# Token sums by six loads, turned norms' last features doubled by DMA, and a new instruction order

## The chip, the cores and the metric

The kernel runs on one core of a Trainium2 chip. The metric is device time in microseconds (us) of one execution; the time before is a median of 681.16 us over three runs (681.0 to 682.04).

## The reference

One transformer block over 2048 tokens of 448 features, float32 in and out: a layer norm, sliding-window attention with 16 heads of 28 features, the residual, a second layer norm, a gated feed-forward of 1792, and the residual.

```
qkv = layernorm(x) @ wqkv                     # 16 heads, Dh = 28
scores = q k^T * Dh**-0.5, kept where 0 <= i - j < 256
h = x + (softmax(scores) v) @ wo
n = layernorm(h)
out = h + (gelu(n @ w_gate) * (n @ w_up)) @ w_down
```

## The kernel before, in words

**Arithmetic.** Each matrix product is made from a high part (the value rounded to the matmul's short float32 form, `to_hi`, on ScalarE, ACT) and a low part (the rest, `to_lo`, a subtraction on VectorE, DVE, or GpSimd, POOL). The features lie on partitions: 448 of them are three blocks of 128 and one of 64, and the fourth block holds the last 64 features' high and low parts one above the other, so that one product is 11 matmuls (`TERMS`) rather than 12 or more.

**Stages.** Tokens come in 16 tiles of 128. Stage one normalises each tile (`layer_norms`, kind `ln1`), transposes it on TensorE (PE), and makes values (`wv`) and queries and keys (`wqk`, `project`); these go to DRAM and return as the operands of the scores in the tile `ring`. Attention runs over blocks of queries: matmuls into PSUM banks (`scores`), a row maximum on DVE (`maxima`), exponentials on ACT (`probs`), a mask on POOL (`select`), products with the values (`attend`), the output weights (`wos`, `ohl`) and the residual (`drain`). There are 256 scores, counted from 0 below, and 16 groups of `attend`.

**The second norm.** `normalise` with kind `ln2` goes through `turn`: DVE transposes 32x32 blocks, four DMAs write the tile to a DRAM scratch (`xn_d`) as features by tokens, and for tiles 0 to 7 two loads bring it back to `xT`, blocks 4 to 6 and block 3. ACT then makes the high parts and POOL (tiles 0 to 3, `TURNED`) or DVE the low parts.

**The feed-forward.** A part of it is done by plain products (`conv`: 22 matmuls of gate and up, a gelu `ge` on ACT, a product on DVE at L1115, high and low parts; `down`: products with the down weights into four banks, which DVE adds to `hres`, L1069). The other part multiplies sums of token tiles with sums of weight columns. `combine(p, i, key)` builds those token sums for a pair of tiles, 4 apart in a half p: it loads both tiles' features from `xn_d` into two scratch rows of blocks `T[0]` (four blocks) and `T[1]` (six), adds and subtracts blocks on DVE (`add`, L460) and writes high parts (`parts_of`, ACT) and low parts (`sub`, DVE, L254) of the sums `X` and `XL`. Pairs 0 to 3 (p = 0) are built while `conv` runs; PE uses the first sum at 360.35 us of the profiled execution.

**Order.** Nothing is scheduled by hardware or by the compiler. Every operation is recorded in `Lists.op` with its engine and what it reads and writes; `play` then emits all of them in an order that the table `PLAN` gives, a packed list of numbers. Each engine, and the DMA queue of SyncE (SP), works through its own list in that order and waits on semaphores, so what stands behind a waiting instruction on its engine waits too. `cost` and `lat` in `op` and `dma` feed only the search that made the table.

Names of tiles in the rows below: `bank_134` to `bank_141` are PSUM banks; `xT`, `ring`, `proj`, `v`, `raw`, `mask` are stretches of SBUF that different stages share; `xn_118` to `xn_133` are the DRAM scratch of the turned tiles 0 to 15.

Of the kernel before, what the change touches and what calls it, by code (L numbers as in the profile page):

```python
# [13 lines left out]
OP = mybir.AluOpType  # L14
# [38 lines left out]
MOVED = 0  # L53
# [82 lines left out]
def block_kernel(ctx: ExitStack, tc, x, wqk_in, wv_in, wo_in, ffn_in, halves_in, out):  # L136
# [57 lines left out]
    last_hi = ring_m[:, 10240:10368]  # L194
# [108 lines left out]
    def normalise(t, key, kind):  # L303
        moved = kind == "ln2" and t >= MOVED
        i2, i4 = (t % 2 if t > 7 else 1) if moved else t % 2 if t < 4 else 1, t % 4
# [44 lines left out]
    def turn(t, key, i2):  # L350
# [8 lines left out]
        if t > 7:  # L359
            return  # L360
        put = [("xnd", t, a) for a in range(4)]
        dma(key + 0.1, 230, lambda: nc.sync.dma_start(f(xT[:, 4:7, c]), d[0:384].rearrange("(b p) t -> p b t", p=128)),
            put, [XT(t)])
        dma(key + 0.1, 80, lambda: nc.sync.dma_start(f(xT[:, 3, c]), d[D - 128:D]), put, [("xt3", t)])

        eng = nc.gpsimd if t in TURNED else nc.vector
# [10 lines left out]
        op("act", 1.1, 1.2, key + 0.2, hi, [("xt3", t)], [XT(t), span("ring", 10240, 128)])  # L377
        op("pool" if t in TURNED else "dve", 1.6 if t in TURNED else 0.8, 1.7 if t in TURNED else 0.88, key + 0.2, lo,
           [XT(t), span("ring", 10240, 128)], [XT(t)], port=True)
# [35 lines left out]
    def combine(p, i, key):  # L415
# [17 lines left out]
        def some(src, *ks):  # L433
            return src[128 * ks[0]:128 * ks[0] + 64 * ks[1]].rearrange("(k p) t -> p k t", k=ks[1])

        for k in range(2):
            t = 8 * p + 4 * k + i
            d, put = xn_d[t], [("xnd", t, a) for a in range(4)]

            def load(rows, lo, n, src, part, k=k, put=put):  # L440
                dma(key, (64 if rows.stop - rows.start == 128 else 32) * n, lambda: nc.sync.dma_start(  # L441
                    T[k][rows, 128 * lo:128 * (lo + n)].rearrange("p (k t) -> p k t", k=n), src), put,
                    [("Th", p, k, part), *at(k, *range(lo, lo + n))])
# [22 lines left out]
        def parts_of(q, src, r, n, key):  # L466
# [21 lines left out]
        add(128, b(1, 2, LOW), at(1, 2), b(0, 2, LOW), at(0, 2), b(1, 4, LOW), at(1, 4), key + 1)  # L488
# [114 lines left out]
    def wqk_split(m):  # L603
# [3 lines left out]
        op("dve", 0.6, 0.7, key, lambda: to_lo(wqk[i][:, 1], wqk_raw[m % 2], wqk[i][:, 0]),  # L607
# [367 lines left out]
    def term(p, j, name, a):  # L975
# [5 lines left out]
        return R[part][:, w, wb], lambda: X(p, q)[:, xb] if xb < 2 else XL(p, LO_OF[q][xb - 2])[:, 0], XS(p, q, xb) + at(part, w, 1, (wb,))  # L981
# [330 lines left out]
    "c-pPEW3(nc)HWEWQb-|H)wXThwr$(CZQHhO+qP|M`t3gbeBaEPHS=TU)Vh;OvT^Mzd)G-IV1NS*2%x{;!0#6Re*Zg$zgOVz2mg^lzklp^3xBsb"  # L1312
    ";sJkt;P>p`(Z8PjmO_7Y|Mvf*`9F64XM`f=z@IVrqrv_>e<kRj+5gd?zvcdVq`xhKKYqy{fAG&d_@e{<=;J@=(VsQ&#}bH`!4adstLRUBC;}b("
    "^Ts3Q!5=2je~3W@A{^o4A8zy;5B{^lBY631`7h?bT;T})e+Xa%p1-`I2#J3&|K)}KLBjsnA%A55vGw;4|B-=zbpKia5%Gfv6fDB~|M2l||NgS|"
    "KNd-ZZ~n)_U%7wU@ITxC=6D1LID$P8p^YODvOl}b{`g=KdkZ4?<PrS;;|NArVi7U&h*kQ>Cye0kACG^v@E@(eZ}^W5{9h)q2(;{v^k1BR{qX<d"
    "LJ^vOc_k6~0wP-YM;1i1C_?X_#9vNW1bg&9-#8-w!5_~&Vt@X|^)LHb1S$~W8AovPH>=Q}>fjL>{=a83`rqmR{KpB7u!$n_@b6y!MT8=%^RHF@"
    "pG6oE`~Rv}9<fh2B9H&^#Utv1L~zCa%To~H^<U5b+t<Ij@h^-1Y0!uo{2MQb(EJx2`mf?yM2-IA|6gUI{~`o`kdg>Ie>wP97dT@4@4NE9zC-^a"
    "XAy7w4@d03JwtzTfJWrsUo_;uYK0Ni^|$|Da{p=#{9jg3#J3Cn;g0@qasS`R{h#gqzsvuBk^49L|4$x+1i$-4zelnDjAH+hiV4yIA4CD^L2?iS"
    "WcaO>0;B{PL0k|55b6K<$plh?tRMiXL1vH*WCtcl403`jzx^f!X+REOf!zNW8}&ea&;T?9jX-121SABxKw1zL<oUgn1pEqrg_S^MPz6*4)j)Mn"
    "1JneyKwgj^L<btk_j|nni1xc}3Yvj}AQ@-{T7x#AEocV{f%c#S=m<K2=AZ@W3~GaEunuSmx`1w=JE#kKfS#ZX=mn<3K|p}PU<jB2b<i6O1riJc"  # L1320
    "rNM9z8O($ufB{B=S#T5>4HiQei~*Cu6fhPng;T*aP!UWA6Tmny8_obT!7Q)@T6i`X4+?`hU@ox1GS~-5+!xG&^MLa^>Ls8U=n9sCg<w8h2Ihn1"
# [174 lines left out]
```

## Time and profile before

| | us |
|---|---|
| median of three runs | 681.16 |
| the profiled execution | 680.14 |
| its span, first to last instruction | 678.4 |
| PE busy | 665.5 (98%) |
| DVE busy | 504.8 (74%) |
| ACT busy | 396.8 (58%) |
| POOL busy | 299.9 (44%) |
| DMA moved | 89.66 MB, 132 GB/s on average |

The profile shows one execution of the program. An engine is busy while it executes; the spans of matmuls overlap, since they are pipelined, and their ends are modelled. PEld is TensorE's loading of weights, which runs ahead of the matmuls. SPq is SyncE's queue, which issues all DMAs of this kernel. In the chain of waits each piece is the work to which the next piece had to wait, followed back from the last instruction. Stages by time: first norm and projections from 8.97 us, first score at 41.08, last `attend` up to 306.69, first sum used at 360.35, and the feed-forward without a gap from 374 to 674.

### The profile page before, as it was taken

The page shows a single profiled execution, that of the slowest core. Times are in us where ns is not written, and L with a number is a line of the kernel's source. Part 1 is how long each engine was busy: PE and PEld are TensorE (multiplying, and loading weights), DVE is VectorE, ACT ScalarE, POOL GpSimd, SP SyncE. Part 2 cuts the span into 40 slices and gives each one's busy share as a digit, 9 for nine tenths or more (in the row PEclk, how much of TensorE's full clock was granted, in tenths as well). Part 3 has the DMA queues.
Part 4 walks back from the last instruction along what each step waited for, and adds up shares of the span by engine and source line. Part 5 has one row for each costly group of instructions (what it writes and reads, how often), then busy time and mean ns, then how long its engine had stood idle before and what let it go on. Part 6 is the DMA issues. An engine that isn't in the chain of part 4 may idle for free.

```text
span 678.4 us, 11973 instructions
## 1 busy us (share of the span) xinstructions
PE 665.5 (98%) x4074; PEld 592.7 (87%) x4074; DVE 504.8 (74%) x1278; ACT 396.8 (58%) x765; POOL 299.9 (44%) x459
## 2 busy tenths in 40 slices
PE   8999999999999999999989999999999999999997
PEld 7998878888889877778878999999999999999997
DVE  7898789977688979977988899876566355545554
ACT  5766578774867698886455655634554443433431
POOL 3632524543444488756433474256554442122200
PEclk9999999999999999999998999999999999999999
DMA  7888866464747687544534434121212201101202
GB/s 268 267 254 250 265 185 210 140 213 135 236 131 255 180 210 221 125 119 105 150 98 95 102 85 128 57 91 39 67 53 70 74 15 52 52 7 62 110 0 109
DMA packets 92951, 89.66 MB, mean 132 GB/s; under 512 B 35225, under 2 KB 82009, under 8 KB 92889
## 3 DMA queue, kind: packets, MB, share of 16 engines
q1 hardware_dynamic: 92888, 88.89, 44.2%
q8 instruction: 32, 0.52, 0.3%
q14 instruction: 31, 0.25, 0.1%
HBM read 59.51 MB, written 29.36 MB: 131 GB/s over the span
## 4 chain that ended last, share of the span: by engine, by line
PE 88%; DVE 7%; DMA 2%; issue 1%; ACT 1%; SPq 1%; POOL 0%; DVEq 0%; ACTq 0%
PE bank L248 81%; PE bank L798 6%; DVE bank L692 2%; DVE v L460 1%; DMA v<-xn 1%; PE bank L314 1%; DMA pp<-in_wv_dram 1%; DVE xT L254 1%; DVE X L254 1%; SPq L441 0%; DVE proj L254 0%; PE bank L719 0%; DVE hres L1069 0%; DVE mhl L712 0%; DVE xn L823 0%
## 5 line engine op out<-in xcount | busy, mean ns | idle before, releaser
L248 PE MATMUL bank<-xT,proj 128*128 128x512 f32 x620 | 171.1, 384 | 0.0
L692 DVE CUSTOM_DVE_ANT_0 bank<-bank,mask 128x384 f32<-128x384 f32 (+2 forms) x256 | 131.6, 551 | 24.0 <-PE bank L248 22.0
L248 PE MATMUL bank<-ring 84*128 84x384 f32 (+6 forms) x618 | 136.3, 311 | 2.4 <-DVE mx L692 1.0
L248 PE MATMUL bank<-xT,ring 128*128 128x512 f32 x536 | 134.8, 379 | 0.0
L248 PE MATMUL bank<-ring,proj 128*128 128x448 f32 x628 | 128.9, 356 | 2.5 <-DVE hres L1069 2.5
L248 PEld LDWEIGHTS bank<-ring,proj 128*128 128x128 f32 x628 | 119.6, 190 | 5.8 <-ACT xT L251 2.9
L248 PEld LDWEIGHTS bank<-xT,proj 128*128 128x128 f32 x620 | 113.6, 190 | 11.4 <-DVE mhl L709 0.2
L766 ACT ACTIVATE pp<-bank 128x384 f32<-128x384 f32 (+1 forms) x212 | 103.3, 533 | 21.6 <-PE bank L248 18.4
L248 PEld LDWEIGHTS bank<-ring 128*128 128x128 f32 (+1 forms) x618 | 103.5, 190 | 13.7 <-DVE mx L692 2.4
L248 PEld LDWEIGHTS bank<-xT,ring 128*128 128x128 f32 x536 | 101.1, 189 | 13.1 <-DVE v L1013 0.6
L779 POOL TENSOR_SCALAR_AFFINE_SELECT pp<-pp 128x512 f32<-128x512 f32 x120 | 73.9, 642 | 56.1 <-ACT pp L766 55.2
L1069 DVE TENSOR_TENSOR hres<-bank,hres 128x448 f32<-128x448 f32 x72 | 42.7, 618 | 33.0 <-PE bank L248 32.9
L248 PE MATMUL bank<-proj,xT 128*128 128x224 f32 x352 | 60.8, 274 | 0.3 <-ACT proj L251 0.2
L937 POOL TENSOR_TENSOR raw<-raw 64x128 f32<-64x128 f32 (+1 forms) x90 | 48.3, 549 | 28.7 <-DMA raw<-in_halves_dram 25.4
L254 DVE TENSOR_TENSOR proj<-v,proj 128x512 fp32r<-128x512 f32 (+1 forms) x56 | 40.2, 725 | 23.9 <-ACT proj L251 23.5
L248 PEld LDWEIGHTS bank<-proj,xT 128*128 128x128 f32 x352 | 52.9, 191 | 2.3 <-ACT proj L251 0.7
L251 ACT ACTIVATE proj<-v 128x512 fp32r<-128x512 f32 (+1 forms) x56 | 32.8, 601 | 36.0 <-DVE v L1039 32.4
L254 POOL TENSOR_TENSOR ring<-raw,ring 128x256 fp32r<-128x256 f32 (+2 forms) x42 | 38.3, 920 | 35.2 <-ACT ring L251 34.5
L251 ACT ACTIVATE ring<-bank 8x512 fp32r<-8x512 f32 x64 | 37.4, 585 | 26.8 <-PE bank L719 25.5
L1013 DVE TENSOR_TENSOR v<-v,bank 128x512 f32<-128x512 f32 x48 | 32.8, 684 | 26.2 <-PE bank L248 23.6
L248 PE MATMUL bank<-wos,ohl 128*128 128x448 f32 x192 | 49.4, 359 | 0.3 <-DVE mx L692 0.2
L248 PE MATMUL bank<-X,ring 128*128 128x512 f32 x146 | 48.2, 379 | 0.0
(117 smaller groups left out, 955.7 us busy)
## 6 DMA issues: line engine op xcount, KB each, us to landing
ring<-k SPq DMA_DIRECT2D x44, 336.0 KB
raw<-in_halves_dram SPq DMA_DIRECT2D x18, 640.0 KB
ring<-q SPq DMA_DIRECT2D x32, 336.0 KB
q<-proj SPq DMA_DIRECT2D x15, 448.0 KB
k<-proj SPq DMA_DIRECT2D x11, 448.0 KB
hres<-in_x_dram SPq DMA_DIRECT2D x16, 224.0 KB
xn<-xn SPq DMA_DIRECT2D x64, 56.0 KB
ge<-in_halves_dram SPq DMA_DIRECT2D x16, 224.0 KB
```

The lines of the kernel that those rows point to most:

```text
L248: nc.tensor.matmul(o.rearrange("p (t h) -> p t h", h=2), w, mixed(m), **how)
L251: nc.scalar.activation(dst, src, AF.Copy)
L254: (eng or nc.vector).tensor_sub(dst, src, f(hi))
L314: nc.tensor.transpose(bank[b.k][:, n * 128:(n + 1) * 128], xn[i2][:, o:o + 128], ident)
L460: op("dve", 0.07 + n * 0.00104, 0.17 + n * 0.00104, key, lambda: nc.vector.tensor_tensor(out, a, b, op=op_), [*ar, *br, "mtfree"], w, port ...
L692: nc.vector.tensor_tensor_reduce(at, at, plain(mask[:, o:384]), 1.0, -BIG, OP.add, OP.max, mx[i // 2][:, i % 2, j:j + 1])
L766: nc.scalar.activation(pp[:, j:j + per, o * 128:o * 128 + n].rearrange("p j (h t) -> p j h t", h=2), bank[b.k][:, 0:n * per].rearrange("p ...
L779: nc.gpsimd.affine_select(a, a, pattern=[[0, 4], [-cm, 128]], compare_op=op_, fill=0.0, base=0, channel_multiplier=cm)
L798: nc.tensor.matmul(bank[b.k][32 * j:32 * j + DH + 1, lo * 128:(hi + 1) * 128], v[:, 4 * c - 2 + m, g % 2, j, :], pp[:, j, at[m] * 128:(at[ ...
L937: op("pool", 0.14 + n * 0.00215, 0.18 + n * 0.00215, key, lambda: nc.gpsimd.tensor_tensor(out, a, b, op=OP.subtract), [*ar, *br], w, port= ...
L1013: op("dve", 0.605, 0.702, key, lambda: nc.vector.tensor_tensor(plain(out), plain(a), unmixed(bank[bs[i].k]), op=OP.add), ar, w, bs[i])
L1069: op("dve", 0.533, 0.626, key + 3 * q + 3, lambda t=t, b=banks[q]: nc.vector.tensor_tensor(plain(hres[:, t, :]), unmixed(bank[b.k][:, 0:D] ...
```

## The change

1. `combine` loads a pair of tiles by six DMAs instead of eight. Features 0 to 383 come by one load of three blocks, and the last 64 features come twice, onto both halves of the partitions, by one load whose source repeats (`twice`). The blocks in `T` change places for it, and so do the weights' rows on the host (`four`) and the order of `X`'s two blocks (`1 - xb`).
2. In `turn` the last 64 features are loaded twice, onto 128 partitions, into 128 columns of `ring`; the high parts of block 3 are then one ACT instruction instead of two.
3. The low parts of the first value weights (`wv_split`, p = 0) and of the first query and key weights (`wqk_split`, m = 0) are made on POOL instead of DVE.
4. `MOVED` goes from 0 to 16 with the test turned round: as before, all tiles of `ln2` take `turn` and none of `ln1` does. The costs in `dma` change, and the table `PLAN` is a new one. 26 warm-up matmuls stand in it instead of 30; the other matmuls are the same.

```diff
     def normalise(t, key, kind):
-        moved = kind == "ln2" and t >= MOVED
+        moved = kind == "ln2" or t >= MOVED
...
     def turn(t, key, i2, kind):
...
-        dma(key + 0.1, 80, lambda: nc.sync.dma_start(f(xT[:, 3, c]), d[D - 128:D]), put, [("xt3", t)])
+        dma(key + 0.1, 80, lambda: nc.sync.dma_start(last, d[D - 64:D][None].to_broadcast([2, 64, 128])), put, [last_at])
...
         def hi():
             to_hi(xT[:, 0:3, c], f(xT[:, 4:7, c]))
-            to_hi(last_hi[64:128], f(xT[64:128, 3, c]))
-            to_hi(xT[0:64, 3, c], f(xT[64:128, 3, c]))
+            to_hi(xT[:, 3, c], last)
 
         def lo():
             to_lo(xT[:, 4:7, c], f(xT[:, 4:7, c]), xT[:, 0:3, c], eng)
-            to_lo(xT[64:128, 3, c], f(xT[64:128, 3, c]), last_hi[64:128], eng)
+            to_lo(xT[64:128, 3, c], last[64:128], xT[64:128, 3, c], eng)
...
     # combine
-            load(slice(0, 128), 0, 2, d[0:256].rearrange("(k p) t -> p k t", k=2), 0)
-            last = d[384:448].rearrange("(k p) t -> p k t", k=1)
-            if not k:
-                load(LOW, 2, 2, some(d, 2, 2), 1)
-                load(HIGH, 2, 2, some(d, 2, 3)[:, 0::2], 2)
-            else:
-                load(LOW, 3, 1, some(d, 2, 2)[:, 1:2], 1)
-                load(LOW, 4, 2, some(d, 2, 2), 2)
-                load(HIGH, 4, 2, some(d, 2, 2), 3)
-                load(HIGH, 2, 2, last.to_broadcast([64, 2, 128]), 4)
+            def twice(r):
+                return d[r:r + 64][None].to_broadcast([2, 64, 128])
+            load(slice(0, 128), 1 + 2 * k, 3, d[0:384].rearrange("(k p) t -> p k t", k=3), 0)
+            load(slice(0, 128), 0, 1, twice(384), 1)
+            if k:
+                load(HIGH, 1, 2, d[0:128].rearrange("(k p) t -> p k t", k=2), 2)
+                load(LOW, 1, 1, d[0:64], 3)
...
-        add(128, b(1, 0), at(1, 0), b(0, 0), at(0, 0), b(1, 0), at(1, 0), key + 1)
+        add(128, b(1, 4), at(1, 4), b(0, 2), at(0, 2), b(1, 4), at(1, 4), key + 1)
...
     # wv_split, for p = 0, and wqk_split, for m = 0
-            op("dve", 0.54, 0.63, key + 1, lambda b=b: to_lo(wv[:, 1, b:b + 2], wv_raw[p][:, b:b + 2], wv[:, 0, b:b + 2]),
+            eng, name = (nc.vector, "dve") if p else (nc.gpsimd, "pool")
...
 PLAN = (
-    "c-pPEW3(nc)HWEWQb-|H)wXThwr$(CZQHhO+qP|M`t3gbeBaEPHS=TU)Vh;OvT^Mzd)G-IV1NS*2%x{;!0#6Re*Zg$zgOVz2mg^lzklp^3xBsb"
...
```

**PE, the end of attention.** Between the last two groups of `attend` (`bank<-pp,v`), before; `bank<-ring` are scores, `bank<-xT,proj` are 512-column matmuls of the feed-forward that need no exponential.

```order
L248 MATMUL bank_135<-ring 128x384
L248 MATMUL bank_141<-xT,proj 128x512
L248 MATMUL bank_135<-ring 128x384
L248 MATMUL bank_137<-ring 128x384
L248 MATMUL bank_134<-ring 128x384
L248 MATMUL bank_140<-ring 128x384
L248 MATMUL bank_135<-xT,proj 128x512 x11
L798 MATMUL bank_139<-pp,v 29x128 x4
L798 MATMUL bank_139<-pp,v 29x256 x4
L798 MATMUL bank_139<-pp,v 29x384 x8
L798 MATMUL bank_139<-pp,v 29x256 x4
```

And the same place after:

```order
L248 MATMUL bank_135<-ring 128x256 x2
L248 MATMUL bank_137<-xT,proj 128x512
L248 MATMUL bank_141<-ring 128x256 x2
L248 MATMUL bank_136<-xT,proj 128x512 x3
L248 MATMUL bank_140<-ring 128x384
L248 MATMUL bank_141<-ring 128x256 x2
L248 MATMUL bank_140<-xT,proj 128x512 x11
L248 MATMUL bank_141<-xT,proj 128x512 x11
L248 MATMUL bank_135<-xT,proj 128x512 x6
L799 MATMUL bank_139<-pp,v 29x128 x4
L799 MATMUL bank_139<-pp,v 29x256 x4
L799 MATMUL bank_139<-pp,v 29x384 x8
```

Between those two groups stood 22 matmuls `bank<-xT,proj` of 512 columns; now there are 58.

**DVE, ahead of the four drains** (`hres<-bank`) in the second half of the first feed-forward part; `v<-v`, `mask<-v`, `X<-v,xT` are the token sums of `combine`. Before:

```order
L254 TENSOR_TENSOR proj<-ge,proj 128x512
L254 TENSOR_TENSOR X_3702<-v,xT 128x2x128
L460 TENSOR_TENSOR v<-v 128x128 x2
L1069 TENSOR_TENSOR hres<-bank_138,hres 128x448
L1069 TENSOR_TENSOR hres<-bank_139,hres 128x448
L1069 TENSOR_TENSOR hres<-bank_140,hres 128x448
L254 TENSOR_TENSOR X_3702<-v,xT 128x128
L254 TENSOR_TENSOR X_3702<-v,xT 128x2x128
L1069 TENSOR_TENSOR hres<-bank_141,hres 128x448
L254 TENSOR_TENSOR X_3702<-v,xT 128x2x128
```

After:

```order
L458 TENSOR_TENSOR v<-mask,v 128x2x128
L254 TENSOR_TENSOR X_3716<-v,xT 128x2x128
L254 TENSOR_TENSOR proj<-ge,proj 128x512
L1070 TENSOR_TENSOR hres<-bank_138,hres 128x448
L1070 TENSOR_TENSOR hres<-bank_139,hres 128x448
L1070 TENSOR_TENSOR hres<-bank_140,hres 128x448
L1070 TENSOR_TENSOR hres<-bank_141,hres 128x448
L458 TENSOR_TENSOR v<-v 128x128
L458 TENSOR_TENSOR v<-v 64x128
L254 TENSOR_TENSOR X_3716<-v,xT 128x2x128
```

The four drains now stand together, directly behind the low part `proj<-ge`, and the sums that stood between come before and after. Counted from the product ahead of that low part (`ge<-bank_135` before, `ge<-bank_137` after), the first drain was the 24th instruction and is now the 18th.

**SP's queue, loads of the third pair** (tiles 2 and 6: `xn_120`, `xn_124`) and the start of the fourth (3 and 7). Before:

```order
L441 DMA v<-xn_124 64x128
L358 DMA xn_126<-xn_80 32x14x32
L441 DMA v<-xn_120 64x2x128
L441 DMA v<-xn_124 64x2x128 x2
L441 DMA v<-xn_124 128x2x128
L441 DMA v<-xn_120 64x2x128
L441 DMA v<-xn_120 128x2x128
L441 DMA v<-xn_125 64x2x128
L931 DMA v<-in_halves_dram 128x448
L441 DMA v<-xn_121 64x2x128
L441 DMA v<-xn_125 64x128
L441 DMA v<-xn_121 128x2x128
```

After:

```order
L442 DMA v<-xn_124 128x3x128
L442 DMA v<-xn_125 128x1x128
L442 DMA v<-xn_124 64x2x128
L442 DMA v<-xn_120 128x3x128
L442 DMA v<-xn_120 128x1x128
L358 DMA xn_126<-xn_80 32x14x32
L442 DMA v<-xn_124 64x128
L442 DMA v<-xn_125 128x3x128
L442 DMA v<-xn_125 64x2x128
L442 DMA v<-xn_125 64x128
L442 DMA v<-xn_121 128x3x128
L442 DMA v<-xn_121 128x1x128
```

Loads of 64 partitions with two blocks give way to one of three blocks (`128x3x128`) and one doubled block (`128x1x128`) for each tile.

More of the change, by code (lines that the diff above doesn't have):

```diff
@@ L52 @@
 PKX = (2, 3)
-MOVED = 0
+MOVED = 16
 QUICK = 4
@@ L193, in block_kernel @@
     xT = xT_m.rearrange("p (b t) -> p b t", b=7)
-    last_hi = ring_m[:, 10240:10368]
+    last = f(ring_m[:, 10240:10368])
     rq_m, rk_m = ring_m[:, 0:4096], ring_m[:, 4096:10240]
@@ L303, in normalise @@
     def normalise(t, key, kind):
-        moved = kind == "ln2" and t >= MOVED
-        i2, i4 = (t % 2 if t > 7 else 1) if moved else t % 2 if t < 4 else 1, t % 4
+        moved = kind == "ln2" or t >= MOVED
+        i2, i4 = t % 2 if t < 4 and kind == "ln1" or t > 7 and kind == "ln2" else 1, t % 4
         b = None if moved else Bank(kind)
@@ L358, in turn @@
             dma(key, 150, lambda dst=dst, src=src: nc.sync.dma_start(dst, src), [at], [("xnd", t, a)])
-        if t > 7:
+        if kind == "ln2" and t > 7:
             return
         put = [("xnd", t, a) for a in range(4)]
+        last_at = span("ring", 10240, 128)
         dma(key + 0.1, 230, lambda: nc.sync.dma_start(f(xT[:, 4:7, c]), d[0:384].rearrange("(b p) t -> p b t", p=128)),
             put, [XT(t)])
-        dma(key + 0.1, 80, lambda: nc.sync.dma_start(f(xT[:, 3, c]), d[D - 128:D]), put, [("xt3", t)])
-        eng = nc.gpsimd if t in TURNED else nc.vector
+        dma(key + 0.1, 80, lambda: nc.sync.dma_start(last, d[D - 64:D][None].to_broadcast([2, 64, 128])), put, [last_at])
+        on_pool = kind == "ln1" or t in TURNED
+        eng = nc.gpsimd if on_pool else nc.vector
         def hi():
             to_hi(xT[:, 0:3, c], f(xT[:, 4:7, c]))
-            to_hi(last_hi[64:128], f(xT[64:128, 3, c]))
-            to_hi(xT[0:64, 3, c], f(xT[64:128, 3, c]))
+            to_hi(xT[:, 3, c], last)
         def lo():
             to_lo(xT[:, 4:7, c], f(xT[:, 4:7, c]), xT[:, 0:3, c], eng)
-            to_lo(xT[64:128, 3, c], f(xT[64:128, 3, c]), last_hi[64:128], eng)
-        op("act", 1.1, 1.2, key + 0.2, hi, [("xt3", t)], [XT(t), span("ring", 10240, 128)])
-        op("pool" if t in TURNED else "dve", 1.6 if t in TURNED else 0.8, 1.7 if t in TURNED else 0.88, key + 0.2, lo,
-           [XT(t), span("ring", 10240, 128)], [XT(t)], port=True)
+            to_lo(xT[64:128, 3, c], last[64:128], xT[64:128, 3, c], eng)
+        op("act", 0.8, 0.9, key + 0.2, hi, [last_at], [XT(t)])
+        op("pool" if on_pool else "dve", 1.6 if on_pool else 0.8, 1.7 if on_pool else 0.88, key + 0.2, lo,
+           [XT(t), last_at], [XT(t)], port=True)
     LOW, HIGH = slice(0, 64), slice(64, 128)
@@ L440, in load @@
             def load(rows, lo, n, src, part, k=k, put=put):
-                dma(key, (64 if rows.stop - rows.start == 128 else 32) * n, lambda: nc.sync.dma_start(
-                    T[k][rows, 128 * lo:128 * (lo + n)].rearrange("p (k t) -> p k t", k=n), src), put,
+                out = T[k][rows, 128 * lo:128 * (lo + n)]
+                if n > 1:
+                    out = out.rearrange("p (k t) -> p k t", k=n)
+                dma(key, (64 if rows.stop - rows.start == 128 else 32) * n, lambda: nc.sync.dma_start(out, src), put,
                     [("Th", p, k, part), *at(k, *range(lo, lo + n))])
-            load(slice(0, 128), 0, 2, d[0:256].rearrange("(k p) t -> p k t", k=2), 0)
-            last = d[384:448].rearrange("(k p) t -> p k t", k=1)
-            if not k:
-                load(LOW, 2, 2, some(d, 2, 2), 1)
-                load(HIGH, 2, 2, some(d, 2, 3)[:, 0::2], 2)
-            else:
-                load(LOW, 3, 1, some(d, 2, 2)[:, 1:2], 1)
-                load(LOW, 4, 2, some(d, 2, 2), 2)
-                load(HIGH, 4, 2, some(d, 2, 2), 3)
-                load(HIGH, 2, 2, last.to_broadcast([64, 2, 128]), 4)
+            def twice(r):
[5 more added lines that the diff above has]
+                load(LOW, 1, 1, d[0:64], 3)
         def add(n, out, w, a, ar, b, br, key, op_=OP.subtract):
@@ L606, in wqk_split @@
         op("act", 0.53, 0.64, key, lambda: to_hi(wqk[i][:, 0], wqk_raw[m % 2]), [WQKRAW(m % 2)], [WQK(i, 0)])
-        op("dve", 0.6, 0.7, key, lambda: to_lo(wqk[i][:, 1], wqk_raw[m % 2], wqk[i][:, 0]),
+        eng, name = (nc.vector, "dve") if m else (nc.gpsimd, "pool")
+        op(name, 0.6 if m else 1.25, 0.7 if m else 1.3, key, lambda: to_lo(wqk[i][:, 1], wqk_raw[m % 2], wqk[i][:, 0], eng),
            [WQKRAW(m % 2), WQK(i, 0)], [WQK(i, 1)], port=True)
@@ L980, in term @@
         part = "lo" if part else "hi"
-        return R[part][:, w, wb], lambda: X(p, q)[:, xb] if xb < 2 else XL(p, LO_OF[q][xb - 2])[:, 0], XS(p, q, xb) + at(part, w, 1, (wb,))
+        return R[part][:, w, wb], lambda: X(p, q)[:, 1 - xb] if xb < 2 else XL(p, LO_OF[q][xb - 2])[:, 0], XS(p, q, xb) + at(part, w, 1, (wb,))
     def whole(*names):
@@ L1317 @@
[L1317 to L1321, printed above, removed]
@@ L1438 @@
+    "ToJAe7lf<A)!~|OZMZI6A8rUYhMU68;g)buxHa4sZVz{ad&8aKuJAy(J3JB|4fln|!h_-Q@I-hhJQ<z}Plsp1!{OQRTzEd*A6^JAhL^(2;g#@e"
+    "crCmWUJq}CH^Y13t?+JmJA4q{4<Ch(!-wJj0=am8QU"
 )
```

274 lines of the change are left out of this document (139 added, 135 removed).

## Prediction

> **What bounds the kernel now.** I read the page first, then busy time by stretch, then the waits, and last the chain of waits around the longest stall.
>
> ```profile
> PE 665.5 (98%) x4074; PEld 592.7 (87%) x4074; DVE 504.8 (74%) x1278; ACT 396.8 (58%) x765; POOL 299.9 (44%) x459
> PE 88%; DVE 7%; DMA 2%; issue 1%; ACT 1%; SPq 1%; POOL 0%; DVEq 0%; ACTq 0%
> ```
>
> TensorE (PE) is busy for 98% of the span and is 88% of the chain that ended last. No engine's total decides, then; the places where PE waits or is fed thinly do. Busy time by stretch (length, then PE, PEld, DVE, ACT, POOL busy with counts, granted clock, DMA share, GB/s):
>
> ```profile
> 0.00:41.08 41.08, 38.38 (x249) 35.01 (x250) 33.84 (x73) 27.62 (x47) 20.67 (x49) 1.00 0.81 264
> 85.00:90.00 5.00, 4.37 (x23) 3.13 (x23) 4.66 (x18) 3.99 (x8) 0.52 (x1) 1.00 0.24 86
> 90.00:238.00 148.00, 147.81 (x1191) 129.48 (x1189) 122.01 (x406) 103.58 (x209) 66.46 (x94) 1.00 0.64 190
> 238.00:306.00 68.00, 65.49 (x530) 52.21 (x532) 57.82 (x175) 59.80 (x127) 52.02 (x78) 1.00 0.65 168
> 353.60:360.40 6.80, 4.26 (x16) 3.62 (x15) 6.72 (x17) 4.14 (x8) 2.68 (x3) 0.79 0.03 10
> 374.00:674.00 300.00, 300.00 (x1461) 275.65 (x1460) 191.33 (x345) 136.11 (x256) 115.27 (x176) 1.00 0.21 63
> 674.00:678.40 4.40, 0.38 (x2) 0.03 (x1) 1.31 (x3) 0.00 (x0) 0.00 (x0) 0.99 0.55 209
> ```
>
> The feed-forward stage (374 to 674) has no gap, so nothing in it can be won without fewer matmuls. Late attention (238 to 306) is where the vector engines are fullest: ACT 59.80 of 68 (88%), DVE 57.82 (85%), against 70% and 82% in the 148 us ahead of it. PE is idle for 68.00 − 65.49 = 2.51 us there. Its weight loads, which run ahead of the matmuls, wait more; first four rows of 238 to 306, then two of 90 to 238 (total us, times, longest):
>
> ```profile
> PEld bank L248 <- DVE mx L692: 2.2, 7, 0.6
> PEld bank L248 <- ACT pp L766: 1.9, 6, 0.9
> PEld bank L248 <- ACT ring L251: 1.0, 2, 0.8
> PEld bank L719 <- ACT v L251: 0.8, 1, 0.8
> ...
> PEld bank L248 <- DVE mx L692: 0.4, 2, 0.3
> PEld bank L248 <- ACT pp L766: 0.4, 1, 0.4
> ```
>
> These four sum to 5.9 us in 68, where the like rows give 0.8 in 148. So late attention loses 2.5 to 5.9 us on vector engines. The other large loss is one stall. The chain from the last attend on (start, us, what):
>
> ```profile
> 306.69 17.65 PE bank L248 x86
> ...
> 324.46 0.60 SPq L441
> ...
> 325.11 0.59 SPq L441
> ...
> 325.75 2.38 DMA v<-xn
> ...
> 331.92 1.89 DMA v<-xn
> ...
> 343.96 0.58 SPq L441
> ...
> 344.58 0.61 SPq L441
> ...
> 345.24 2.21 DMA v<-xn
> ...
> 355.91 0.55 DVE hres L1069
> ...
> 356.59 5.49 PE bank L248 x18
> ```
>
> Behind 17.65 us of PE work the chain belongs to `combine`: its loads (the queue's issues, then some 2.2 us to land) and DVE's sums, until a drain of four banks at 355.91 lets PE go on at 356.59. PE is idle for 6.80 − 4.26 = 2.54 us, and then runs 18 matmuls in 5.49 us, 0.305 each. At the feed-forward's pace of 300.00/1461 = 0.205 us they take 3.7, so 1.8 us more goes to the lowered clock (0.79 in this stretch). The stall costs 4.3 us.
>
> **The change, part by part.**
>
> *Prices by width.* In 374 to 674 the 1461 matmuls are 575 of 448 columns (next row) and 886 of 512; time by columns gives 300.00/(575·448 + 886·512) = 0.42 ns a column, so 0.216 us for 512, 0.189 for 448, 0.095 for 224.
>
> ```profile
> L248 PE MATMUL bank<-ring,proj 128*128 128x448 f32 x575 | 116.0, 352 | 0.0
> ```
>
> *The new order, late attention.* From scores 192 to the last attend the order holds 105 filler matmuls of 512 columns for 77, and 88 of 224 for 44: 28 × 0.216 + 44 × 0.095 = 10.2 us more that needs no exponential. It stands where the weight loads wait. The loss is 2.5 to 5.9, and I put it at 4.8, above the middle, since waits below 0.2 us are not listed. A sixth of it I leave standing: the last groups still begin with scores. Term −4.0; bounds 0 (ACT and DVE themselves set the pace) and −5.9.
>
> *The new order, 85 to 90.* 23 matmuls in 5.00 us; at the pace of the next stretch (147.81/1191 = 0.124) they need 2.9. Idle 0.63, stretched 2.1. DVE (4.66 of 5.00) sets it, and the new order has 1.3 us more PE work between scores 64 and 95. Term −0.8; 0 to −2.1.
>
> *The new order, early.* That filler comes from elsewhere. Priced by width, PE has 30.0 us of work ahead of its first score (41.08), where it had 35.8; DVE has 2.1 us less ahead of it. DVE is busy 33.84 of those 41.08 us, 7.2 free. If DVE's chain sets the first score, PE loses up to 5.8 − 2.1 = 3.7; if the free time takes it up, 0. Between scores 96 and 127 PE has 23.8 us for 30.6; DVE's list there outweighs PE's in one dozen scores, by 8%, under 1 us. PE led the chain in both places, so I take +1.0 for them; 0 to +4.7.
>
> *Six loads, not eight.* Eight pairs of tiles; four fall before the first sum is used (360.35), the others beside the gapless feed-forward, where 2 us more or less changes nothing. In the four, SP issues 8 fewer at 0.58 to 0.61 us. Two stretches of the chain end in such issues (324.46 to 325.75, 343.44 to 345.24), each two fewer at 0.6: −2.4. The new loads have no row of their own: the nearest is `v<-xn` in the chain, 1.89 to 2.38 us, which I take for them. Below that bound nothing is left to gain, since fewer bytes don't land sooner than 1.89; the upper bound is the rival on queues, below.
>
> *The sums' arithmetic* has the same number of instructions and sizes; only blocks change place. DVE's list between the first product of raw values and the last sum shrinks, as the order moves other work out. In the trace:
>
> ```profile
> 312.22:360.35 48.13, 45.34 (x216) 41.33 (x215) 43.18 (x105) 25.92 (x48) 20.60 (x30) 0.97 0.46 120
> ```
>
> 105 instructions, 43.18 us; after it is 92, at the same mean of 0.411 us 37.8: −5.4. Against it, PE's cover behind the last attend falls from 362.2 to 356.2 us of work (all matmuls by width), −6.0, and the raw products come 1.1 us of work later. So 1.1 + 6.0 − 5.4 − 2.4 = −0.7 on a stall of 4.3. The four drains now stand together, right behind the product's low part, with the sums after them; that holds the value down if anything. Term −0.7; −4.3 to +4.
>
> *Turned norms.* One DMA for one, and two ACT instructions for three, eight times:
>
> ```profile
> L251 ACT ACTIVATE xT<-xT x16: 307/410/570, 242.9 to 304.5; 128x384 fp32r<-128x384 f32 x8, 64x128 fp32r<-64x128 f32 x8
> L251 ACT ACTIVATE ring<-xT x8: 306/307/308, 243.5 to 304.2; 64x128 fp32r<-64x128 f32 x8
> ```
>
> Two of 0.307 become one as wide, on more partitions: 0.3 × 8 = 2.4 us less of ACT's 59.80. It is part of the −4.0. The doubled block now lands in the ring, one buffer, so each load waits on SP's queue for the low part of the tile before, with score loads (L669) behind it. At present only the last tile's loads are waited for, by ACT 0.6 and so by DVE 3.2:
>
> ```profile
> ACT xT L251 <- DMA xT<-xn: 0.6, 1, 0.6
> DVE xT L254 <- ACT xT L251: 3.2, 1, 3.2
> ```
>
> I take 0 for it, with +2 as the upper bound for a longer landing at that last tile, and −0.6 as the lower.
>
> *First weights on POOL.* Three low parts leave DVE for POOL; the nearest rows are 0.73 us there and 1.14 to 1.31 here:
>
> ```profile
> L254 DVE TENSOR_TENSOR proj<-v,proj 128x512 fp32r<-128x512 f32 (+1 forms) x56 | 40.2, 725 | 23.9 <-ACT proj L251 23.5
> ...
> L254 POOL TENSOR_TENSOR ring<-raw,ring x3: 1142/1311/1737, 305.5 to 308.2; 128x512 fp32r<-128x512 f32 x2, 128x448 fp32r<-128x448 f32 x1
> ```
>
> ```profile
> 2.65 5.11 DMA pp<-in_wv_dram
> ...
> 8.97 0.81 PE bank L248 x5
> ```
>
> PE starts real work at 8.97, behind a weight load and two ACT copies, and its chain is its own from there, so POOL's longer time is hidden behind the high parts' matmuls: 0. Without that cover each low part costs its 0.6 more, +1.8; the lower end is −0.7, one DVE part that PE no longer meets. Four fewer warm-up matmuls: 0.
>
> **Sum.** −4.0 − 0.8 + 1.0 − 0.7 = −4.5 on the profiled execution, 680.14 (its span 678.4 and 1.74 around it), so 675.6. The median of the three runs, 681.16, lies 1.0 above that execution; against it the forecast is **676.7 us**.
>
> **Rivals.**
>
> *A. The close gives it back.* The 2.4 us of the loads are hidden behind DVE, which has other sums in its list; then the close is 1.1 + 6.0 − 5.4 = +1.7, and the time 676.7 + 2.4 = 679.1. For it: between the last product ahead of the drains and the drains DVE had next to no free time. Against: two loads sat on the chain.
>
> ```profile
> 347.14:355.83 8.69, 6.91 (x34) 5.99 (x32) 8.52 (x24) 2.89 (x6) 3.85 (x5) 1.00 0.42 102
> ```
>
> *B. Late attention is the vector engines' own.* ACT at 88% and DVE at 85% cannot be helped by PE filler if they are a chain. Then −4.0 becomes 0: 680.7, no change. Against: 70% and 82% in the stretch ahead ran without a stall, and ACT loses 2.4 us.
>
> *C. All three stalls go.* −5.9 − 2.1 − 4.3 with +1.0 and the rest zero, −11.3 in full, and some of each will stay, so about −10: 671.
>
> *D. The doubled loads run on two DMA engines; slower.* The new source puts the two copies outermost, `[2, 64, 128]` with a step of nothing. Before, a repeat stood in the middle and 64 or 128 partitions outermost. If the work is dealt out along that first dimension, 64 KB go through two engines of 16. The peak in the close (third of these slices on is `v<-xn`) is 349 GB/s, 22 an engine:
>
> ```profile
> GB/s 0 0 0 71 349 210 54 117 78 146 180 112 170 349 251 127 114 116 124 76 77 136 149 137 98 0 68 176 107 91 41 157 343 46 0 0 0 8 39 0
> ```
>
> Sixteen engines move 64 KB in 0.19 us, two in 1.5: 1.3 us later for one load, 2.6 for the second of two in a row. The close has eight, the turned norms eight. From 3.5 exposed ones on (4.5/1.3) the gain is gone; with six in the close uncovered it is +7.8, 684.5. Against: in the new order DVE has 11 to 38 instructions (at 0.411, 4.5 to 15.6 us) between what frees the buffer and the load's first reader; issue and landing need 0.6 × 2 to 4 plus 2.2, so only the first pair lacks the slack. No row of before shows such a load. The Trainium skill, page "DMA: Bandwidth & Descriptors", sections "Why a DMA increments its semaphore by 16 and not by 1" and "Rules for kernel authors", states this: the number of engines follows the slowest dimension that isn't one, and a leading zero-stride broadcast of c copies confines the DMA to at most c. By it each doubled load has D's price, and the sum is 676.7 plus 1.3 for each that nothing covers; no run here shows it yet.
>
> **Chances.** The forecast 0.42, A 0.2 (three quarters of it still faster), B 0.1, C 0.1, D 0.18. A measurement of this kernel can tell about 0.2%, 1.4 us. Faster: 0.42 + 0.15 + 0.1 and a little of B, 0.68; same: the rest of A, most of B, 0.13; slower 0.19. The range takes C's centre and D's: **671 to 684.5**; beyond lie half of C and half of D, 0.14.
>
> **What would show it.** Late attention: PE idle below 1.2 us in its last 68 us, and weight-load waits on `mx` and `pp` below 2. Close: a stall ahead of the drains (L1070) of 1 to 2.5 us instead of 2.54, and clock 1.00 behind it if below. Early: first score near 36 to 39 us instead of 41.08. D: `v<-xn` of 128x1x128 and `ring<-xn` landing after 3 us or more, with DVE or ACT waiting on them by name. The forecast is wrong if ACT stays above 85% with PE idle over 2 us there, or if the last sum comes later than 355 us.

## The result, and the profile after

The changed kernel takes 688.32 us (median of six runs, 687.81 to 689.47) against 682.14 us for the kernel before in the same comparison: a ratio of 1.0085, with a 95% interval of 1.006 to 1.011. It is slower by 0.85%, and outside the range. Its profiled execution took 687.87 us, span 686.2. From its page, first busy time, then shares of the chain that ended last:

```profile
PE 665.9 (97%) x4070; PEld 590.6 (86%) x4070; DVE 499.8 (73%) x1275; ACT 393.9 (57%) x757; POOL 296.2 (43%) x462
...
PE 79%; DVE 11%; DMA 4%; ACT 2%; issue 2%; SPq 1%; POOL 1%; DVEq 0%; ACTq 0%; POOLq 0%
```

PE's work is the same; DVE has a larger share of the chain (11% for 7) and DMA twice its share (4% for 2). Busy time by stretch (length, then PE, PEld, DVE, ACT, POOL with counts, clock, DMA share, GB/s), first the changed kernel:

```profile
85.00:90.00 5.00, 5.00 (x35) 4.78 (x34) 4.96 (x16) 4.46 (x10) 4.59 (x7) 1.00 0.40 138
255.00:277.00 22.00, 19.89 (x195) 15.42 (x194) 18.61 (x58) 17.55 (x36) 16.44 (x25) 1.00 0.86 224
345.00:362.00 17.00, 14.18 (x69) 12.65 (x68) 16.05 (x45) 9.55 (x18) 5.34 (x8) 1.00 0.23 70
404.00:445.00 41.00, 36.27 (x167) 30.73 (x166) 34.17 (x79) 21.64 (x42) 17.40 (x27) 1.00 0.29 87
```

and the kernel before, in two of these stretches:

```profile
404.00:445.00 41.00, 41.00 (x200) 37.37 (x199) 36.03 (x80) 22.01 (x42) 18.06 (x28) 1.00 0.30 87
345.00:362.00 17.00, 14.46 (x64) 12.99 (x63) 16.18 (x42) 9.18 (x19) 7.12 (x10) 0.90 0.28 72
```

The stretch from 404 to 445, where PE had no gap, now has 4.73 us of it. That is where `combine` builds the second half's sums. The chain of waits there, in time:

```profile
433.81 4.24 DMA v<-xn
...
438.70 0.43 DVE mask L458
...
439.45 0.54 DVE X L254 x2
...
440.34 4.84 PE bank L248 x20
```

The load is one of 64 partitions, 32 KB, that reports 16 times; it takes 4.24 us from its issue. It stands in the queue behind two doubled loads, issued at 431.48 and 432.75, which landed at 435.53 and 437.40. Then DVE makes sums, and then PE goes on. The waits of that stretch (total us, times, longest):

```profile
DVE v L458 <- DMA v<-xn: 5.5, 3, 2.0
...
ACT xT L251 <- DMA v<-xn: 4.0, 2, 3.7
```

In the whole execution ACT waits for the turned norms' doubled loads too:

```profile
ACT xT L251 <- DMA ring<-xn: 2.9, 2, 2.1
```

The trace also has the moment at which each DMA engine reports the end of its share of a DMA. Worked out from these, by load:

| load | reports a load | last report after the end of its issue, median (least to most), us |
|---|---|---|
| `v<-xn`, before, 64 | 16 | 1.75 (1.54 to 3.97) |
| doubled `v<-xn`, after, 16 | 3 | 3.56 (3.29 to 6.04) |
| doubled `ring<-xn`, after, 8 | 3 | 3.42 (3.06 to 6.83) |
| other `v<-xn`, after, 32 | 16 | 2.92 (1.54 to 4.91) |

A doubled load reports three times: once at 0.42 us, well ahead of the first report of any other `v<-xn` load (1.2 us), and twice at 3 us or more. I read the last two as two engines that carry the data, which is rival D. The loads on 16 engines are later too, and only in their last two reports: the 14th comes at 2.02 us in the median, the 15th at 2.70 and the 16th at 2.92. With the doubled loads split (below) the same three come at 1.94, 1.97 and 2.04. That fits two engines which have a doubled load in front.

Where PE's time went can be summed from the starts of its matmuls: what an interval to the next start exceeds the pitch of its shape (0.216 us for 512 columns, 0.189 for 448, and so on). The pitches of narrow matmuls are estimates, so the differences between columns count and not the totals. In us:

| stretch | before | after | after, doubled loads split (below) |
|---|---|---|---|
| up to 238, without 85 to 90 | 19.5 | 21.8 | 21.3 |
| 85 to 90 | 1.8 | 0.4 | 0.4 |
| 238 to 313, late attention | 10.1 | 9.3 | 8.4 |
| 313 to 362, first half's sums | 5.0 | 4.2 | 1.5 |
| 362 to 445, second half's sums | 0.4 | 7.6 | 4.8 |
| last matmul to the end | 4.4 | 5.8 | 4.8 |

The columns are single executions, of 680.14, 687.87 and 680.10 us. Of the 5.0 before, 1.7 is not a wait: the clock was at half for 3.41 us behind the stall (357.48 to 360.89), and in the other two executions it was not lowered there.

### The profile page after: what moved, and what is told of

It is laid out like the page before. It is cut to its first block, busy times and chain, and to the rows that moved or that the text cites. A ratio compares the mean times of both kernels' runs of the same rounds, so it can differ in the third digit from the quotient of the medians.

```text
span 686.2 us, 11907 instructions
## 1 busy us (share of the span) xinstructions
PE 665.9 (97%) x4070; PEld 590.6 (86%) x4070; DVE 499.8 (73%) x1275; ACT 393.9 (57%) x757; POOL 296.2 (43%) x462
## 4 chain that ended last, share of the span: by engine, by line
PE 79%; DVE 11%; DMA 4%; ACT 2%; issue 2%; SPq 1%; POOL 1%; DVEq 0%; ACTq 0%; POOLq 0%
PE bank L248 74%; PE bank L799 4%; DVE xT L254 2%; DVE X L254 1%; DVE bank L693 1%; DVE proj L254 1%; DMA k<-proj 1%; DMA raw<-in_ffn_dram 1%; DVE hres L1070 1%; DVE v L458 1%; SPq L648 1%; DMA hres<-in_x_dram 1%; DMA v<-xn 1%; ACT proj L251 1%; DVE bnst L284 1%
## 5 line engine op out<-in xcount | busy, mean ns | idle before, releaser
L693 DVE CUSTOM_DVE_ANT_0 bank<-bank,mask 128x384 f32<-128x384 f32 (+2 forms) x256 | 131.6, 550 | 24.2 <-PE bank L248 21.8
L248 PE MATMUL bank<-ring 128*128 128x384 f32 (+5 forms) x618 | 138.1, 310 | 1.6 <-ACT ring L251 0.8
L248 PEld LDWEIGHTS bank<-xT,ring 128*128 128x128 f32 x536 | 100.7, 189 | 21.3 <-DVE v L1014 2.2
L938 POOL TENSOR_TENSOR raw<-raw 64x128 f32<-64x128 f32 (+1 forms) x90 | 43.3, 491 | 50.4 <-DMA raw<-in_halves_dram 40.4
L248 PE MATMUL bank<-proj,xT 128*128 128x224 f32 x352 | 63.8, 273 | 0.0
L248 PEld LDWEIGHTS bank<-proj,xT 128*128 128x128 f32 x352 | 55.4, 192 | 1.3
```

Source lines behind the costliest of these rows:

```text
L248: nc.tensor.matmul(o.rearrange("p (t h) -> p t h", h=2), w, mixed(m), **how)
L693: nc.vector.tensor_tensor_reduce(at, at, plain(mask[:, o:384]), 1.0, -BIG, OP.add, OP.max, mx[i // 2][:, i % 2, j:j + 1])
L938: op("pool", 0.14 + n * 0.00215, 0.18 + n * 0.00215, key, lambda: nc.gpsimd.tensor_tensor(out, a, b, op=OP.subtract), [*ar, *br], w, port= ...
```

## Experiments

All ratios are to the kernel before, with 95% intervals.

**Splitting the doubled loads.** The order and everything else of the changed kernel stay.

```diff
-            load(slice(0, 128), 0, 1, twice(384), 1)
+            for rows in (LOW, HIGH):
+                nc.sync.dma_start(T[k][rows, 0:128], d[384:448])
...
-        nc.sync.dma_start(last, d[D - 64:D][None].to_broadcast([2, 64, 128]))
+            nc.sync.dma_start(last[0:64], d[D - 64:D])
+            nc.sync.dma_start(last[64:128], d[D - 64:D])
```

> The changed kernel, its order untouched, but each of the 24 doubled loads is two loads of 64 partitions by 128 (both with 64 as the outermost dimension), issued one after the other. Theory Q (queues: a doubled load runs on two DMA engines, lands in 3.3 to 3.6 us instead of 1.6 to 1.8 and holds back what is queued behind it on these two): the 7.2 us that PE loses between the first and the last product of sums go, and the time falls by 6 to 9 us from 688.3, to 679 to 682. Theory O (order: the new table itself leaves the second half's sums too little cover, and the loads are hidden): 688 to 690, since SP issues 24 DMAs more.

Measured: 682.02 us, ratio 1.0003 (0.9989 to 1.0017). All loads report 16 times; the halves land in 1.58 us, the others in 2.04. So 6 us come back although SP issues 24 DMAs more: theory Q. Reading the same rows twice is not what was slow, since the split loads do it too. The load of 4.24 us above, issued at 428.66 here, landed 2.15 us later, and the chain has 1.16 of it:

```profile
428.66 1.16 DMA v<-xn
```

But it comes level with the kernel before, not below it. Of the 7.2 us that Q expected back from the second half, 2.8 came (7.6 to 4.8 in the table); for the rest theory O holds, the new order itself. Its stretches:

```profile
345.00:362.00 17.00, 16.62 (x82) 15.03 (x81) 16.66 (x41) 8.90 (x17) 8.25 (x13) 1.00 0.17 50
404.00:445.00 41.00, 37.66 (x178) 32.74 (x177) 37.79 (x84) 22.91 (x45) 15.07 (x24) 1.00 0.28 80
```

The first half's stall is gone (PE idle 0.38 for 2.54 before), the second half's is still 3.34.

**Splitting those of `combine` alone.** The first part of that diff.

> As the run before, but only the 16 doubled loads of combine are split; the 8 of the turned norms stay doubled. Theory Q with the loss in combine alone: within 1 us of the run with all split. If the turned norms' loads cost something in late attention as well: 1 to 3 us above it. Theory O: 688 to 690.

Measured: 682.67, ratio 1.0006 (0.9994 to 1.0018). The loss sits in `combine`; the turned norms' doubled loads, 3.5 us to land, are covered to within what can be measured.

**Two engines in the kernel before.** 62 partitions divide by no larger number up to 16 than two. Two partitions of the sums are left stale, so the values differ.

```diff
-                load(LOW, 2, 2, some(d, 2, 2), 1)
+                load(slice(0, 62), 2, 2, some(d, 2, 2)[0:62], 1)
...
-                load(LOW, 4, 2, some(d, 2, 2), 2)
+                load(slice(0, 62), 4, 2, some(d, 2, 2)[0:62], 2)
```

> The kernel before, its order untouched; in combine the load of the lower 64 partitions, two blocks, is cut to 62 partitions, once for each tile (16 loads). 62 is two times a prime, so by Q's rule it runs on two engines, 62 packets each, as the doubled loads do; two partitions of sums are left stale, so the values differ. Theory Q: landing 3.2 to 3.6 us and a time 3 to 9 us above before. Theory O: within 0.5 us of before.

Measured: 683.68, ratio 1.003 (1.0015 to 1.0045). The 16 loads report three times and land in 3.17 us (2.83 to 5.24). The chain now has

```profile
325.95 4.72 DMA v<-xn
...
346.68 2.25 DMA v<-xn
```

and PE's waits for the drains, first before, then here:

```profile
PE bank L248 <- DVE hres L1069: 2.8, 2, 2.5
```

```profile
PE bank L248 <- DVE hres L1069: 4.0, 2, 2.5
```

Loads as slow as these thus cost 2 us in the old order and some 6 in the new one. That the new order leaves DVE less other work in front of them is argued, not shown. The size, 3 to 9 us, was missed; the sign and the place were right. With the turned norms' loads on two engines as well (they then bring other rows, so the values differ):

```diff
-        nc.sync.dma_start(f(xT[:, 3, c]), d[D - 128:D])
+        nc.sync.dma_start(f(xT[:, 3, c]), d[D - 192:D].rearrange("(a p) t -> a p t", p=64)[0::2])
```

> As the run before, and the turned norms' loads of block 3 take two lots of 64 rows that are not next to each other (rows 256 to 319 and 384 to 447 instead of 320 to 447, other values in the lower half), so that the outermost dimension is two and they run on two engines. Theory Q: the run with combine alone plus 0 to 3 us. Theory O: within 0.5 us of before.

Measured: 683.04, ratio 1.0016 (0.9998 to 1.0033), not to be told from the run with `combine` alone.

**One load of 128 rows for the doubled one.** Six loads, none on two engines; the lower halves then hold other features, so the values differ.

```diff
-                return d[r:r + 64][None].to_broadcast([2, 64, 128])
+                return d[r - 64:r + 64]
...
-        nc.sync.dma_start(last, d[D - 64:D][None].to_broadcast([2, 64, 128]))
+        nc.sync.dma_start(last, d[D - 128:D])
```

> The changed kernel, six loads and its order untouched, but each doubled load brings 128 consecutive rows (320 to 447) instead of 64 rows twice: same bytes, one DMA, but the outermost dimension is 128 (the lower halves hold other features, so the values differ). Theory Q: it lands in 1.6 to 2.2 us on 16 engines and shows what the change is worth without the two engines: 679 to 682, SP's queue being shorter than with split loads by 24 issues of 0.5. If the six loads as such gain nothing: 681.5 to 682.5. Were it not the engines but the repeated reading of the same rows that is slow: 681 to 682 as well, and the split loads would tell, which read them twice too and were quick.

Measured: 682.59, ratio 1.002 (1.0003 to 1.0036). With 16 reports each and 2.0 us to land, six loads in the new order are no faster than eight in the old one. Two loads fewer for each pair, my −2.4, are worth nothing to be seen. Why it lies a little above the split version is open; in its profiled execution the clock was lowered for 3.4 us in late attention, which neither the changed kernel nor the split version had there.

**What holds the second half's sums.** The adds and subtractions of blocks on POOL, by `ADDS`, and then left out.

```diff
-ADDS = ("dve", "dve")
+ADDS = ("dve", "pool")
```

> The changed kernel with all doubled loads split, and in combine's second half (p = 1) the 24 adds and subtractions of blocks on POOL instead of DVE, in the same order. In the run with all split PE loses 4.7 us between 404 and 445 us, where DVE is busy 30.1 of 32 us. Theory V (DVE's list sets the pace up to the last token sum): some 5.9 us leave DVE, the stalls at 412 and 432 us go or shrink to under 1.5, and the time is 678 to 679.5, that is 3 to 4 us below 682.0. Theory L (the second half waits for its loads and buffers): stalls stay, 681.5 to 683.5, POOL being slower for each.

Measured: 682.41, ratio 1.0005 (0.9989 to 1.0022). Theory V's gain did not come. In 404 to 436, first with DVE's adds, then with POOL's:

```profile
404.00:436.00 32.00, 28.66 (x135) 24.57 (x133) 30.09 (x68) 17.32 (x34) 13.93 (x22) 1.00 0.30 89
```

```profile
404.00:436.00 32.00, 29.68 (x137) 24.87 (x135) 27.94 (x51) 17.82 (x35) 23.86 (x36) 1.00 0.32 92
```

DVE has 17 instructions fewer but only 2.15 us less busy time. The 17 adds took 7.23 us (records of neighbours overlap), but the 51 instructions that stay take 30.40 us for 27.02, so 0.60 on average for 0.53. That the busier POOL slows them is likely, but not shown. And the chain now runs through POOL:

```profile
422.63 0.97 POOL v L458
...
423.68 1.33 POOL v L458 x2
```

With the first half's adds on POOL (`("pool", "dve")`):

> As the run before, but the adds of the first half (p = 0) go to POOL and those of the second stay on DVE. Theory V, one list up to the last sum: the first sum is used 0 to 1 us earlier, and DVE starts the second half earlier, so that the stalls at 412 and 432 shrink by 1 to 3 us: 679 to 681.5. Theory L, or a second half that cannot start earlier: stalls stay at 3.5 to 4.7, 681.5 to 683.

Measured: 686.58, ratio 1.0059 (1.004 to 1.0078): the first half's loss returns, 4.6 us between 345 and 362, of which 1.7 is a lowered clock. With both:

> All doubled loads split, and the adds of both halves on POOL. Theory V: as with the second half alone or up to 1 us better, 677.5 to 679.5. Theory L: 682 to 685, with POOL's waits added.

Measured: 686.54, ratio 1.0061 (1.0042 to 1.0079). Both are above what either theory gave. And in the kernel before, both:

> The kernel before, with the adds of both halves on POOL. Theory V: the stall of 2.54 us ahead of the drains at 356 us and the lowered clock behind it go or halve, and since DVE has 11 us less in all, nothing is given back later: 677 to 680 against 682.0. Theory L: the stall stays, 681.5 to 684.

Measured: 682.43, ratio 1.0002 (0.9987 to 1.0017). The loss between 313 and 362 fell from 5.0 to 3.3, and 2.8 appeared between 362 and 445, where there had been 0.4. The fall is no gain of POOL's: it is the lowered clock, 1.7 us, which this execution did not have, and PE's idle time is about the same. The stretch before, then here:

```profile
313.00:362.00 49.00, 46.22 (x218) 42.00 (x217) 44.03 (x108) 26.05 (x49) 21.36 (x31) 0.97 0.44 111
```

```profile
313.00:362.00 49.00, 46.42 (x226) 42.26 (x226) 41.36 (x83) 27.37 (x51) 32.74 (x54) 1.00 0.46 122
```

So V's gain did not come in the old order either. With POOL for the first two pairs of the second half only (`if p and i < 2` in `add`):

> All doubled loads split, and of combine's second half only the adds of the first two pairs on POOL. Theory V: 3 us leave DVE where their lateness is covered, the stalls at 412 and 432 shrink by 1 to 3 us: 679 to 681.5. Theory W: no change, 681.5 to 683.

Measured: 682.33, ratio 1.0021 (1.0002 to 1.0039): no gain. Left out altogether, so that the sums are stale and the values differ:

```diff
+            if p:
+                op("dve", 0.07 + n * 0.00104, 0.17 + n * 0.00104, key, lambda: None, [*ar, *br, "mtfree"], w, port=True)
```

> All doubled loads split as before, and the 24 adds and subtractions of blocks of combine's second half left out (their sums are stale values, so the values differ); everything else in its place. Theory V (DVE's own work sets the second half): 9 us of DVE work go without any on POOL, the stalls at 412 and 432 us vanish, and the time is 677 to 679. Theory W (each pair waits for its loads and for the one set of buffers, DVE only ends that chain): 2 us or more of the 4.7 stay, 680 to 681.5.

Measured: 680.35, ratio 0.9986 (0.9963 to 1.0008). The loss between 404 and 445 fell from 4.7 to 2.3:

```profile
404.00:436.00 32.00, 30.83 (x145) 26.64 (x144) 27.30 (x55) 19.01 (x38) 13.24 (x21) 1.00 0.30 89
```

So in this execution about half is DVE's own work, as V says, and half stays without it, as W says; neither alone. It is the fastest of ten, 677.79 us, and the interval of the ratio takes in 1, so the medians show less than the trace. Which wait makes the half that stays is open.

**What holds late attention.** Masked maxima on half their columns in the last four blocks of queries.

```diff
-            at = unmixed(bank[b.k][:, o:384])
+            o2 = (o + 384) // 2 if B >= 12 else o
+            at = unmixed(bank[b.k][:, o2:384])
```

> All doubled loads split, and the masked maxima of the last four blocks of queries (64 of 256) on half their columns (the values differ). It asks what sets late attention, where PE loses 6.8 us between 262 and 313. If DVE's runs of maxima do (12 in a row at 0.52 us between 264 and 272): PE's loss there falls by 2 to 4 us and the last attend comes that much earlier; the time falls by less, 679.5 to 681.5, as the second half's sums give some back. If ACT's exponentials do: less than 0.7 us, 681.5 to 682.5.

Measured: 678.71, ratio 0.9972 (0.9953 to 0.999), less than I expected. The loss between 262 and 313 fell from 6.8 to 4.6, and the second half's sums gave nothing back (4.7 as before). The stretch in the split version, then with halved maxima:

```profile
255.00:277.00 22.00, 20.12 (x197) 15.68 (x195) 18.19 (x58) 18.87 (x39) 16.37 (x25) 1.00 0.82 223
```

```profile
255.00:277.00 22.00, 21.36 (x204) 16.98 (x204) 15.17 (x59) 19.68 (x41) 17.41 (x26) 1.00 0.84 221
```

PE's idle time there goes from 1.88 to 0.64 as DVE's busy time goes from 18.19 to 15.17, while ACT's rises: DVE's maxima set most of it. What sets the 4.6 that stay between 262 and 313 is open. With 12 of 16 blocks halved, in the kernel before (`if c else o`):

> The kernel before, with the masked maxima on half their columns in 12 of the 16 blocks of queries (the shift of the exponent is then not the row's true maximum). DVE loses some 45 us of work in attention. If DVE's runs of maxima set the waits of attention in the order of before as well: PE's loss between 238 and 306 falls by 3 us or more, that at 85 to 90 stays, and the time is 677 to 679.5. If ACT and the chain of matmul, exponential and product set them: 680.5 to 682.

Measured: 677.58, ratio 0.9927 (0.9902 to 0.9953). The time is as expected of DVE but PE's loss between 238 and 313 fell by 2.1 rather than 3. And in the split version:

> All doubled loads split, and the same maxima halved. With those of the last four blocks halved it was 678.7, PE losing 4.6 us between 262 and 313 for 6.8. If the earlier blocks' maxima hold PE up too: 676.5 to 678.5. If only the last four do: 678.3 to 679.5. If it comes out level with the kernel before so halved, the new order is worth nothing there; 1 us or more below it, the order helps attention once DVE is relieved.

Measured: 677.36, ratio 0.9927 (0.9904 to 0.9949). From 238 on, before and then split:

```profile
238.00:306.00 68.00, 66.73 (x549) 53.75 (x548) 49.39 (x177) 61.55 (x130) 53.37 (x79) 1.00 0.64 169
```

```profile
238.00:306.00 68.00, 67.31 (x507) 57.22 (x509) 44.79 (x159) 54.85 (x115) 48.45 (x70) 1.00 0.64 167
```

With DVE relieved, the new order loses 5.8 us in late attention (238 to 313) and the old one 7.9; but behind it the new one loses 5.5 between 362 and 445 and the old one 0.4. They come out level again. Both beat the two kernels of this case, but only by shifting the exponent by something other than the row's maximum, which holds as long as no score outside the half lies far above those within it.

## Why the prediction was wrong, point by point

The forecast was 4.5 us faster and the kernel came out 6.2 us slower, a miss of 10.7. Two steps of the sum make it: the price of the doubled loads, some 6 us, and the second half's sums, put at nothing, 4.4 us with split loads. The other terms' errors nearly cancel.

**The loads (the first step that failed).** "the nearest is `v<-xn` in the chain, 1.89 to 2.38 us, which I take for them." A row of the same name was no price for a load of another shape: with some 0.5 us of issue, as in those rows, the doubled loads of `combine` took 4.1 in the median. Rival D had the rule, and its 1.3 us a load was somewhat low: from the end of the issue 3.56 against 1.75 is 1.8. Its signs came, DVE and ACT waiting for `v<-xn` and `ring<-xn` by name. Its place was half right: of the loss that splitting takes away, 2.7 lies in the close and 2.8 in the second half, which D did not count, and the turned norms' eight cost nothing that can be measured. The price is settled by splitting the loads (6 us back) and by 62 partitions in the old kernel. I held D to 0.18 because "only the first pair lacks the slack". The slack was counted in DVE instructions between the buffer's release and the load's first reader; but ACT reads too, the queue holds other loads, and those on 16 engines came 0.9 us later in the median (2.92 for 2.04), which D's sum left out. The Trainium skill, page "DMA: Bandwidth & Descriptors", section "Rules for kernel authors", says that a leading zero-stride broadcast of c copies confines a DMA to at most c engines; the trace agrees, with two reports of data for c = 2.

**"the others beside the gapless feed-forward, where 2 us more or less changes nothing" (the second).** A stretch without a gap can be one without slack. DVE was busy 36.03 of its 41 us before. The new order reaches 404 us some 5 us ahead once the loads are split, and loses 4.7 of that by 445; with doubled loads, 7.6. This term stood at zero; about half of it with split loads is DVE's work, by the run without adds, and the rest is open.

**Late attention, −4.0.** The mechanism was right in part, the size wrong: −1.7 with split loads, −0.8 in the changed kernel. In the 68 us up to the end of its last `attend` the changed kernel has

```profile
244.60:312.60 68.00, 65.47 (x504) 53.54 (x502) 48.67 (x148) 50.97 (x108) 47.46 (x69) 1.00 0.61 160
```

The weight loads' waits on `mx` and `pp` fell to 1.5 us each, below the 2 that I named, but PE is idle 2.53 us for 2.51 before, not below 1.2. "It stands where the weight loads wait" failed. The 58 matmuls between the last two groups stand from 292 to 310; PE's idle time between 255 and 277 rose to 2.11 in the changed kernel (row shown with the result) from 0.95 before:

```profile
255.00:277.00 22.00, 21.05 (x188) 16.21 (x187) 21.19 (x71) 19.28 (x42) 19.34 (x29) 1.00 0.75 215
```

Runs of maxima keep DVE there, as the halved ones show. My rival B blamed the vector engines in general; it was DVE, and ACT, busy 50.97 of 68 us, was not the bound.

**The close of the first half, −0.7.** With split loads −3.5, with doubled ones −0.8. That the −0.8 lies beside the forecast is luck: PE's idle time there rose, 3.14 us for 2.78 before, and what fell is the lowered clock of 1.7 us. With split loads the idle time is 0.70. The drains put together may have done that, but no run takes them apart. Rival A's +1.7 did not come, but what it doubted, the six loads' −2.4, was indeed nothing to be seen. Of the signs that I gave for being wrong, the last sum later than 355 us came: DVE was still at sums at 359, and PE used the first at 360.56.

**85 to 90, −0.8:** −1.4, the right way and larger. **Early, +1.0:** the first score came at 36.89, as forecast, and PE lost 1.8 to 2.3 more up to 238; the bound of 4.7 held. **First weights on POOL, 0:** no wait of PE shows it. **SP's shorter queue, −2.4:** nothing, by the run with 128 rows. With split loads the stretches sum to −0.4 and the end to +0.4: level, as measured.

## What to carry to other kernels

Look at the outermost dimension of both sides of every new DMA before taking a neighbour's landing time for it: a saved issue of 0.6 us here was bought with 1.8 us of landing, and with later loads behind it. A new order in which PE waits less early is worth only what the vector engines can follow later: price the stretch behind it, even where it has no gap. And place filler work by where an engine waits in time, not by the group to which the waits are booked.

## What the runs showed of the hardware that was not expected

- A DMA on two engines holds up DMAs on 16: their last report moved from 2.04 to 2.92 us in the median, while their first 14 reports hardly moved (the 14th from 1.94 to 2.02).
- A load of 62 partitions reports as on two engines, and one of 64 as on 16: three reports, the last at 3.17 us, against 1.75 for the loads of 64 or 128 partitions.
- Moving 17 DVE instructions to POOL shortened DVE's busy time by 2.15 us only; the mean of the 51 others went from 0.53 to 0.60 us beside a busier POOL (23.86 for 13.93 us of 32). Whether POOL is the cause was not isolated.
- The clock fell to half for 3.41 us in late attention in four of the profiled executions (128 rows, and three of those with adds on POOL), beside idle times of PE of 0.27, 0.54 and 0.81 us within 5 us. With the same gaps it did not fall in the split version or in the changed kernel. At the stall of 2.53 to 2.54 us ahead of the drains it fell in three executions in the old order and not in a fourth (62 partitions). Such an episode costs some 1.7 us, so that much of a difference between single executions says nothing.
